# Loads at the start of a retention, ELU and max-out kernel: keys over all partitions, each weight half loaded once

## The chip, the cores and the metric

The kernel runs on one core of a Trainium2 chip. The metric is the device time of one execution in microseconds (us). Three executions of the kernel before took 1005.8, 998.84 and 1005.3 us, a median of 1005.3 us. A fourth execution was profiled and took 1000.28 us.

## The reference

Three stages follow one another. A retention layer runs over 4 sequences of 768 tokens with 8 heads of 64; its result goes, token by token, through a layer with ELU, and that result through a layer that takes the greatest of three projections.

```python
state = gamma * state + einsum('bhd,bhe->bhde', k[:, :, t], v[:, :, t])
y[:, :, t] = scale * einsum('bhd,bhde->bhe', q[:, :, t], state)
x = y.transpose(0, 2, 1, 3).reshape(3072, 512)
h = x @ moe_w_in                                    # 512 -> 2048
x = where(h > 0, h, exp(minimum(h, 0)) - 1) @ moe_w_out   # 2048 -> 512
h = maximum(maximum(x @ w1, x @ w2), x @ w3)        # 512 -> 768, three times
out = h @ moe2_w_out                                # 768 -> 512
```

The second and third stages' weights arrive as 64-bit numbers and are turned into pairs of 32-bit numbers on the chip.

## The kernel before

Retention runs in chunks of 128 tokens, 24 in all. The ELU layer runs over blocks of 512 tokens and over 16 slices of 128 hidden columns, numbered `f`. Products are made in three passes with a high and a low part of each operand.

**Chunks.** `load(c)` brings one chunk. The first eight (`early`, `EARLY` = 8) come from `qkv0`, where a row has five blocks of 128 numbers: queries of the first head of a pair, queries of the second head (each with zeros in the other head's rows), keys of both heads, keys by token, and values by token. In the tile `x`, slot 0 is for queries, slot 1 for keys, slot 3 for values; `rows(0)` are partitions 0 to 63, `rows(1)` are 64 to 127. Four transfers make up an early chunk: queries of `rows(0)`, keys of `rows(0)`, queries and keys of `rows(1)` in one (lines 110 to 114), and then the values over all partitions (line 127).

**Weight halves.** The 16 slices of the ELU layer's weights are loaded as 32 halves, numbered `n`, each of 128 rows of 4096 bytes (512 KB). `load_half(n)` chooses a place: `stage` (two buffers) or, for n = 2 to 5, a tile of the pool `ld` (two buffers with the tag `r`) that holds two halves, `duo`. A half is turned from 64 to 32 bits in steps: `scale` on ScalarE (line 307), `shift`, `sign` and `tail` on VectorE (lines 311, 317, 323), then `whigh` on ScalarE (line 341) and `wlow` on VectorE (line 346). The temporary `t` of a half has two buffers and is given back by `wlow`. Once `tail` is done, the place of a half is free, and `cv_tail` asks there for a later half (lines 327 and 328). In the first part of the kernel, which runs through `class Early`, `Early.tail` calls `cv_tail` and then asks for the same half itself (lines 1001 and 1002).

**Order.** SyncE (SP) issues all loads of chunks and halves in the order of the program, one after the other; an issue that waits holds back all behind it. The start is written out at line 845: chunks 0 and 1, half 0, chunks 2 and 3, half 1, chunk 4, halves 2 and 3, chunk 5, half 4, chunk 6, half 5, chunk 7. The string `ORDER` then gives the order of all steps of the first part for TensorE (PE), VectorE (DVE), ScalarE (ACT) and GpSimd (POOL); each engine runs its own steps in that order. Halves pass through `tail` in the order 0, 1, 2, 3, 4, 6, 5, 8, 7. Of `ORDER`, the stretch that matters reads:

```
mask6 fade7 scale6 shift6 sign6 tail6 hb2 exp2 relu2 score7:12 update7 mask7 middle7 oa0 oc0 ob0 whigh6
wlow6 ha3:0 hc3 hb3 whigh3 wlow3 scale5 oa1 oc1 ob1 state7 value7:12 near7 elu2 ghigh2 shift5 sign5 tail5
scale8 shift8 sign8 tail8 exp3 relu3 whigh5 oa2 wlow5 scale7 oc2 guard7 far7 high7 elu3 value6:03 near6
```

Here `ha`, `hb`, `hc` are the three passes of the ELU layer's first product for a slice (line 1080), `oa`, `ob`, `oc` those of its second product (line 1088); `turn`, `score`, `update`, `value`, `near`, `far`, `guard`, `mask`, `middle`, `state`, `keys` are steps of retention (`far` on PE is line 248 and its like, `guard` on ACT is line 973, `mask` on DVE line 203, `value` of the later chunks line 261). After `ORDER` the steady loop begins: `h1` (line 376) and `o1` (line 410) by turns.

Of the kernel before, what the change touches and what calls it, by code (L numbers as in the profile page):

```python
# [17 lines left out]
P = 128  # L18
# [13 lines left out]
NSTAGE = 2  # L32
# [25 lines left out]
def kernel(ctx: ExitStack, tc: tile.TileContext, qkv0, qkv, wa, wb, dmask, qdec, cols, out):  # L58
# [34 lines left out]
    def load(c, part=None):  # L93


        if c >= NCHUNK:
            return

        early = c < EARLY
        src = qkv0 if early else qkv  # L100
        if part != 1:
            if c in raw_t:
                return
            if early:
                x = wpool.tile([P, NPAIR, 4, P], F32, tag="w", name="x")
            else:
                x = ld.tile([P, NPAIR, 4, P], F32, tag="r", name="x")
            raw_t[c] = x
            if early:
                for h, at_, o, n in ((rows(0), 0, 0, 1), (rows(0), 1, 2, 1), (rows(1), 0, 1, 2)):  # L110
                    nc.sync.dma_start(
                        out=x[h, :, at_:at_ + n, :].rearrange("d p s t -> d p (s t)"),
                        in_=src[c, :, h, o * P:(o + n) * P].rearrange("p d t -> d p t"),
                    )
            else:
                for g in range(2):
                    for s in range(2):
                        for p in range(1 if c < 2 * NCH else 2):
                            ps = slice(None) if c < 2 * NCH else slice(p, None, 2)
                            cc = slice((2 * s + (g ^ p)) * P, (2 * s + (g ^ p) + 1) * P)  # L120
                            nc.sync.dma_start(
                                out=x[rows(g), ps, s, :], in_=src[c, ps, rows(g), cc].rearrange("p d t -> d p t")
                            )
        if part != 0:
            x = raw_t[c]
            if early:
                nc.sync.dma_start(
                    out=x[:, :, 3, :], in_=src[c, :, :, 4 * P:5 * P].rearrange("p t n -> t p n")
                )
            else:  # L130
                nc.sync.dma_start(
                    out=x[:, :, 2:4, :].rearrange("t p s n -> t p (s n)"),
                    in_=src[c, :, :, 4 * P:].rearrange("p t n -> t p n"),
                )
# [3 lines left out]
    def rows(i):  # L138
        return slice(i * HC, (i + 1) * HC)
# [149 lines left out]

    def load_half(n):  # L290
        if n < len(sources):
            if 2 <= n < 6:
                if n % 2 == 0:
                    duo[n // 2] = ld.tile([P, 2, 512, 2], I32, tag="r", name="raw")
                r = duo[n // 2][:, n % 2]
            else:
                r = stage.tile([P, 512, 2], I32, tag="raw", name="raw")
            nc.sync.dma_start(out=r.rearrange("p n w -> p (n w)"), in_=sources[n].bitcast(I32))
            half[n] = r
# [21 lines left out]
    def cv_tail(n):  # L321
        t = tmp[n].bitcast(U32)
        nc.vector.scalar_tensor_tensor(
            out=t, in0=half[n][:, :, 0].bitcast(U32), scalar=29, in1=t,
            op0=ALU.logical_shift_right, op1=ALU.bitwise_or,
        )
        if n < 2 or n >= 6:
            load_half(n + 6 if n < 2 else n + NSTAGE)

    def cv_rest(n):  # L330
        if n // 2 >= len(keys):
            return
        cv_shift(n)
        cv_sign(n)
        cv_tail(n)
# [179 lines left out]
    def words(src, t, loaded, freed):  # L515
# [20 lines left out]
        def tail():  # L536
# [3 lines left out]
            )  # L540

        get = Op("S", 0.0, load, *loaded)
        got = Op("A", 0.67, scale, (get, 2), *freed)
        Op("D", 0.42, shift, (got, 0))
        Op("D", 0.69, sign)
        return get, Op("D", 0.69, tail)

    def prepare(k, slot, prev):
# [296 lines left out]
    for c, n in ((0, None), (1, 0), (2, None), (3, 1), (4, 2), (None, 3), (5, 4), (6, 5), (7, None)):  # L845
        if c is not None:
            load(c)
        if n is not None:
            load_half(n)
# [19 lines left out]
    class Early:  # L869
# [128 lines left out]

        def tail(n):
            cv_tail(n)  # L1000
            if n < 2 or n >= 6:
                load_half(n + 6 if n < 2 else n + NSTAGE)

        def whigh(n):
            cv_high(n)
# [99 lines left out]
    def visit(c):  # L1105
        if c // CB not in x_t:
            new_x(c // CB)
        values(c)
        load(c + 2)
        open_chunk(c + 1)  # L1110
        finish(c)
        ready(c + 1)
# [15 lines left out]
    n = 2 * FIRST  # L1128
# [191 lines left out]
```

## Time and profile before

| | before |
|---|---|
| three executions | 1005.8, 998.84, 1005.3 us |
| median | 1005.3 us |
| profiled execution | 1000.28 us |
| its span, first to last instruction | 998.2 us |
| PE busy | 980.1 us (98%) |
| DVE busy | 607.1 us (61%) |
| ACT busy | 350.2 us (35%) |
| loads of weight halves | 37 of 512 KB |

A profile's page gives an engine's busy time over the whole span. The first 75 us, in which chunks and weights arrive, differ from the rest: they are the part that the change is in. The views of the trace that show them are the waits of an engine within a window, the chain of work that ended last in order of time, the timeline of one engine, and the table of windows with what the DMA engines moved.

### The profile page before, as it was taken

The page shows a single profiled execution, that of the slowest core. Times are in us where ns is not written, and L with a number is a line of the kernel's source. Part 1 is how long each engine was busy: PE and PEld are TensorE (multiplying, and loading weights), DVE is VectorE, ACT ScalarE, POOL GpSimd, SP SyncE. Part 2 cuts the span into 40 slices and gives each one's busy share as a digit, 9 for nine tenths or more (in the row PEclk, how much of TensorE's full clock was granted, in tenths as well). Part 3 has the DMA queues.
Part 4 walks back from the last instruction along what each step waited for, and adds up shares of the span by engine and source line. Part 5 has one row for each costly group of instructions (what it writes and reads, how often), then busy time and mean ns, then how long its engine had stood idle before and what let it go on. Part 6 is the DMA issues. An engine that isn't in the chain of part 4 may idle for free.

```text
span 998.2 us, 18878 instructions
## 1 busy us (share of the span) xinstructions
PE 980.1 (98%) x7820; PEld 848.6 (85%) x7820; DVE 607.1 (61%) x1137; ACT 350.2 (35%) x672; POOL 73.3 (7%) x84
## 2 busy tenths in 40 slices
PE   9889999999999999999999999999999999999998
PEld 6668887877887888888887888999999999999997
DVE  4766878544456655656654623676585765858654
ACT  2545665423443444444445433122121211212111
POOL 2200001021111111111110101000000000000000
PEclk9999999999999999999999999999999999999999
DMA  9943454344545554565556865402011020110101
GB/s 224 211 162 97 160 158 166 104 128 131 158 134 156 178 182 129 163 196 159 159 163 209 298 206 179 149 1 86 1 44 43 1 85 1 43 43 2 43 1 43
DMA packets 82308, 119.58 MB, mean 120 GB/s; under 512 B 6960, under 2 KB 59184, under 8 KB 79920
## 3 DMA queue, kind: packets, MB, share of 16 engines
q1 hardware_dynamic: 73008, 87.45, 29.8%
q0 software_dynamic: 3024, 19.66, 6.1%
q10 hardware_dynamic: 6192, 11.28, 3.2%
q8 instruction: 61, 1.00, 0.4%
q14 instruction: 23, 0.19, 0.1%
HBM read 84.02 MB, written 34.34 MB: 119 GB/s over the span
## 4 chain that ended last, share of the span: by engine, by line
PE 88%; DMA 6%; DVE 2%; ACT 2%; issue 1%; SPq 0%; ACTq 0%
PE hp L755 27%; PE acc L410 24%; PE hp L376 23%; PE acc L804 10%; DMA raw<-in_wa 3%; DMA x<-in_qkv 2%; PE xs L189 1%; PE xs L248 1%; PE xs L261 1%; PE xs L221 1%; DVE e L387 1%; DMA ops_d<-m 1%; PE bank L1088 1%; ACT gh L388 1%; ACT e L383 0%
## 5 line engine op out<-in xcount | busy, mean ns | idle before, releaser
L755 PE MATMUL hp<-xh,w 128*128 128x256 f32 x1512 | 275.0, 283 | 0.0
L755 PEld LDWEIGHTS hp<-xh,w 128*128 128x128 f32 x1512 | 237.0, 192 | 0.7
L376 PE MATMUL hp<-xh,w 128*128 128x512 f32 x736 | 235.8, 389 | 0.0
L755 PE MATMUL hp<-xl,w 128*128 128x256 f32 x756 | 213.9, 283 | 0.0
L410 PE MATMUL acc<-gh,w 128*128 128x512 f32 x736 | 194.4, 394 | 2.3 <-DVE part L435 0.9
L410 PEld LDWEIGHTS acc<-gh,w 128*128 128x128 f32 x736 | 135.7, 188 | 34.9 <-ACT gh L388 2.5
L376 PEld LDWEIGHTS hp<-xh,w 128*128 128x128 f32 x736 | 138.1, 188 | 28.8
L755 PEld LDWEIGHTS hp<-xl,w 128*128 128x128 f32 x756 | 145.1, 192 | 0.7
L387 DVE SCALAR_TENSOR_TENSOR e<-e,hp 128x512 f32<-128x512 f32 x92 | 63.0, 685 | 131.6 <-ACT e L384 131.2
L376 PE MATMUL hp<-xl,w 128*128 128x512 f32 x368 | 137.3, 389 | 0.0
L410 PE MATMUL acc<-gl,w 128*128 128x512 f32 x368 | 105.1, 390 | 0.0
L762 DVE TENSOR_TENSOR t<-hp,m 128x256 f32<-128x256 f32 (+1 forms) x108 | 55.0, 509 | 75.8 <-PE hp L755 75.3
L383 ACT ACTIVATE e<-hp 128x512 f32<-128x512 f32 x92 | 54.7, 594 | 123.0 <-PE hp L376 121.2
L391 DVE TENSOR_TENSOR gl<-e,gh 128x512 fp32r<-128x512 f32 x92 | 64.2, 698 | 49.0 <-ACT gh L388 47.5
L774 ACT COPY m<-hp 128x256 f32<-128x256 f32 x54 | 20.1, 373 | 198.3 <-PE hp L755 107.5
L388 ACT CAST gh<-e 128x512 fp32r<-128x512 f32 x92 | 57.1, 621 | 91.5 <-DVE e L387 91.5
L804 PE MATMUL acc<-w,gh 128*128 128x512 f32 x288 | 88.9, 390 | 0.0
L410 PEld LDWEIGHTS acc<-gl,w 128*128 128x128 f32 x368 | 69.1, 188 | 15.0 <-DVE gl L391 0.4
L376 PEld LDWEIGHTS hp<-xl,w 128*128 128x128 f32 x368 | 69.1, 188 | 14.4
L804 PEld LDWEIGHTS acc<-w,gh 128*128 128x128 f32 x288 | 54.1, 188 | 10.7
L384 ACT ACTIVATE e<-e 128x512 f32<-128x512 f32 x92 | 58.2, 633 | 2.9
L804 PE MATMUL acc<-w,gl 128*128 128x512 f32 x144 | 56.2, 391 | 0.0
(144 smaller groups left out, 990.7 us busy)
## 6 DMA issues: line engine op xcount, KB each, us to landing
raw<-in_wa SPq DMA_DIRECT2D x37, 512.0 KB, 3.7
w<-ops_d POOLq DMA_DIRECT2D x18, 1024.0 KB, 5.2
ops_d<-m SPq DMA_DIRECT2D x66, 256.0 KB, 3.0
raw<-in_wb SPq DMA_DIRECT2D x24, 512.0 KB, 4.4
x<-in_qkv SPq DMA_DIRECT2D x16, 512.0 KB, 4.3
x<-in_qkv SPq DMA_DIRECT2D x96, 64.0 KB, 2.5
raw<-x2d SPq DMA_DIRECT2D x10, 512.0 KB, 4.3
x<-in_qkv SPq DMA_DIRECT2D x32, 128.0 KB, 4.6
```

The lines of the kernel that those rows point to most:

```text
L189: nc.tensor.matmul(banks[g][rows(s), p, :], x[rows(g), p, 1, t], x[rows(g), p, 0, t], start=p == 0, stop=p == NPAIR - 1, skip_group_check= ...
L376: nc.tensor.matmul(hp, w[:, pw, kk * P:(kk + 1) * P], x[px][:, kk, :], start=k == 0, stop=k == len(order) - 1,)
L383: nc.scalar.activation(e, hp, ACTF.Exp)
L384: nc.scalar.activation(e, e, ACTF.Relu, scale=-1.0, bias=1.0)
L387: nc.vector.scalar_tensor_tensor(out=e, in0=e, scalar=-1.0, in1=hp, op0=ALU.mult, op1=ALU.max)
L388: nc.scalar.copy(gh, e)
L391: nc.vector.tensor_tensor(out=gl, in0=e, in1=f32(gh), op=ALU.subtract)
L410: nc.tensor.matmul(acc_t[b][m], w[:, p[0], 512 + m * P:512 + (m + 1) * P], g[p[1]], start=f == f0 and p == first, stop=f == f1 - 1 and p = ...
L755: nc.tensor.matmul(o, ws[i][:, pw, kk * P:(kk + 1) * P], xs[i][px][:, kk, :], start=first and k == 0, stop=last and k == 5,)
L762: nc.vector.tensor_tensor(out=out, in0=a, in1=c, op=ALU.add)
L774: nc.scalar.copy(u, pa[:, :HB])
L804: nc.tensor.matmul(acc_t[NB + b][m], g[px][:, m * P:(m + 1) * P], w[:, pw, :], start=f == 0 and i == 0, stop=f == KF2 - 1 and i == 2,)
```

## The change

Three edits. In `load`, an early chunk still comes by four transfers, but the cut is another: queries of `rows(0)`, queries of `rows(1)`, and keys over all 128 partitions in one; values as before. A packet is then always one row of 512 bytes, where queries and keys of `rows(1)` came in rows of 1024 bytes.

`Early.tail` no longer asks for a half, so that `cv_tail` alone does.

`load_half` puts halves 8 and 9 into a `duo` tile of the pool `ld`, where halves 2 and 3 were, and `cv_tail` asks for them once half 3 has passed `tail`. Halves 6 and 7 ask for 10 and 11 when they have passed, 8 and 9 ask for nothing, and from 10 on each asks for the one two further, as before. `ORDER` is not changed.

```diff
             if early:
-                for h, at_, o, n in ((rows(0), 0, 0, 1), (rows(0), 1, 2, 1), (rows(1), 0, 1, 2)):
+                for h, at_, o in ((rows(0), 0, 0), (rows(1), 0, 1), (slice(None), 1, 2)):
                     nc.sync.dma_start(
-                        out=x[h, :, at_:at_ + n, :].rearrange("d p s t -> d p (s t)"),
-                        in_=src[c, :, h, o * P:(o + n) * P].rearrange("p d t -> d p t"),
+                        out=x[h, :, at_, :], in_=src[c, :, h, o * P:(o + 1) * P].rearrange("p d t -> d p t")
                     )
...
-            if 2 <= n < 6:
+            if 2 <= n < 6 or n in (8, 9):
...
-        if n < 2 or n >= 6:
-            load_half(n + 6 if n < 2 else n + NSTAGE)
+        if n < 2:
+            load_half(n + 6)
+        elif n == 3:
+            load_half(8)
+            load_half(9)
+        elif n in (6, 7):
+            load_half(n + 4)
+        elif n >= 10:
+            load_half(n + NSTAGE)
...
         def tail(n):
             cv_tail(n)
-            if n < 2 or n >= 6:
-                load_half(n + 6 if n < 2 else n + NSTAGE)
```

## Rows read from the trace of the kernel before

**Rows 1.** The page: the span.

```profile
span 998.2 us, 18878 instructions
```

**Rows 2.** The page, DMA issues: count, KB of each, median us from issue to landing.

```profile
raw<-in_wa SPq DMA_DIRECT2D x37, 512.0 KB, 3.7
```

**Rows 3.** Waits of PE from 5 to 76 us: us in total, times, longest.

```profile
PE bank L1088 <- ACT w L341: 2.2, 1, 2.2
PE bank L984 <- ACT xh L980: 2.1, 2, 1.4
PE bank L221 <- DVE room L203: 1.6, 1, 1.6
PE bank L1088 <- issue: 1.5, 1, 1.5
...
PE bank L873 <- DMA x<-in_qkv: 0.4, 1, 0.4
```

**Rows 4.** Window 90 to 140: length, each engine's busy time (instructions), clock, DMA share, GB/s.

```profile
90.00:140.00 50.00, 50.00 (x222) 41.42 (x221) 39.67 (x67) 30.14 (x53) 0.00 (x0) 1.00 0.45 144
```

**Rows 5.** Chain that ended last, 0 to 80 us: start, us, what (DMA: issue to landing).

```profile
40.38 8.41 DMA raw<-in_wa
48.80 3.98 DMA raw<-in_wa
...
55.46 4.98 DMA raw<-in_wa
...
60.46 3.71 DMA raw<-in_wa
...
64.25 0.66 ACT t L307
...
66.62 2.12 PE bank L1088 x8
```

**Rows 6.** Waits of SP, 0 to 80 us: us in total, times, longest.

```profile
SPq L298 <- DMA raw<-in_wa: 27.5, 6, 7.2
```

**Rows 7.** Timeline of DVE: start, us, what; in brackets the idle time before.

```profile
53.50 0.43 DVE L311 TENSOR_SCALAR t<-t 128x512 int32<-128x512 int32 x1 [0.54 <-ACT t L307]
...
59.60 0.69 DVE L323 SCALAR_TENSOR_TENSOR t<-raw,t 128x512 uint32<-128x512 uint32 x1
64.94 0.43 DVE L311 TENSOR_SCALAR t<-t 128x512 int32<-128x512 int32 x1 [4.64 <-ACT t L307]
```

**Rows 8.** Timeline of ACT, the same columns.

```profile
58.60 0.62 ACT L1034 CAST gh<-e 128x512 fp32r<-128x512 f32 x1 [0.91 <-DVE e L1028]
64.25 0.66 ACT L307 ACTIVATE t<-raw 128x512 f32<-128x512 f32 x1 [5.03 <-DMA raw<-in_wa]
```

**Rows 9.** Timeline of PE, the same columns.

```profile
56.19 0.73 PE L1088 MATMUL bank<-gh,w 128*128 128x512 f32 x2 [1.55 <-issue]
...
59.51 1.07 PE L1080 MATMUL bank<-xl,w 128*128 128x512 f32 x4
...
63.23 0.69 PE L261 MATMUL bank<-room,x 64*64 64x64 f32 x32
```

**Rows 10.** Six windows of the loads, with the columns of rows 4.

```profile
14.00:16.50 2.50, 2.50 (x40) 1.99 (x36) 1.68 (x4) 1.14 (x2) 0.05 (x1) 1.00 1.20 199
16.50:17.50 1.00, 1.00 (x27) 0.93 (x24) 0.97 (x2) 0.47 (x1) 0.23 (x1) 1.00 1.22 255
...
34.30:35.40 1.10, 1.10 (x7) 0.91 (x6) 1.03 (x3) 0.74 (x2) 0.25 (x1) 1.00 1.13 198
21.00:22.80 1.80, 1.80 (x21) 1.44 (x23) 0.98 (x2) 0.00 (x0) 1.19 (x1) 1.00 1.07 320
39.60:41.50 1.90, 1.15 (x48) 1.01 (x48) 1.83 (x3) 0.65 (x2) 0.62 (x1) 1.00 1.14 228
42.00:43.00 1.00, 0.65 (x22) 0.52 (x26) 0.62 (x2) 1.00 (x2) 0.00 (x0) 1.00 1.15 184
```

**Rows 11.** DMA queues from 53 to 56 us: packets, MB, share.

```profile
q8 instruction: 1, 0.02, 2.1%
```

## Prediction

> **What bounds the kernel now.** I read the page first, then PE's waits before and after the start, then the chain in order of time, then the timelines of the engines along that chain, and last the windows of the loads.
>
> The span is 998.2 us [rows 1], and TensorE (PE) is busy in nearly all of it. From 90 to 140 us it is busy for 50.00 us of 50.00 [rows 4]: behind the start, PE's own work sets the pace. So a load counts only where PE waits for it, and time won there moves everything behind it forward by the same amount. PE's waits from 5 to 76 us are seven rows, of which the first four and the last are shown; the seven add up to 9.7 us [rows 3]. This is the ceiling for a change that touches only loads.
>
> Next, what the waits come from. The chain from 40 us on is made of weight halves: one lands at 48.79, the next is issued at 48.80 and lands 3.98 us later, a third is issued at 55.46, and a fourth, issued at 60.46 when the third has landed, lands 3.71 us later, just before ScalarE (ACT) begins `scale8` at 64.25 [rows 5]. By the code these are the first and the second copy of half 6 and of half 8: the first copy's buffer, that nobody reads, is filled again once the transfer is in. The page counts 37 loads of halves [rows 2] where the program has 32 halves; the five too many are the second copies of 6, 7, 8, 9 and 10. The queue of SyncE (SP) waited 27.5 us for earlier halves [rows 6], though that is no cost by itself.
>
> **Second copies, removed.** Half 6 lands about 4 us earlier (48.79 for 52.79). That is worth little: VectorE (DVE) idled only 0.54 us before `shift6` [rows 7], and the steps ahead of it keep it busy. PE waits for none of this, so I cost it at nothing.
>
> Half 8 is the one that counts. Its first copy had to wait for `tail6` and is issued at 55.46. ACT then idled 5.03 us before `scale8` [rows 8]; behind `scale8` in ACT's order stand `exp3`, `relu3` and `whigh5`, and PE's `oa2` at 66.62 waited 2.2 us for `whigh5` [rows 3, 5]. In the changed kernel half 8 goes out behind half 7, since `tail3` is long done. If half 6 lands at 48.79 as its first copy does now, halves 7 and 8 follow at about 1.6 us each (0.524 MB at 320 GB/s [rows 10]), so half 8 is in by 52 us and half 9 by 54. I then follow ACT: `ghigh2` ends at 58.60 + 0.62 = 59.22 [rows 8], `scale8` takes 0.66 and ends at 59.9. `exp3` needs the last matmul of `hb3`, 59.51 + 1.07 = 60.58 [rows 9]. `exp3` and `relu3` take about 0.62 each (as `ghigh2` does) and bring 61.8, by when `tail5` is done (59.60 + 0.69 = 60.29 [rows 7]); `whigh5` ends at 62.4. PE arrives at `oa2` at 66.62 - 2.23 = 64.4, behind `value7` (63.23 [rows 9]) and `near7`. So `whigh5` is 2.0 us early, and the wait goes: **2.2 us**. What is late next on PE is PE itself. DVE's idle 4.64 us before `shift8` [rows 7] goes too, so that `tail8` and `tail7` run ahead of PE. The second copies of 7, 9 and 10 lie on no wait of PE: nothing. What hides them is PE's own products; without these, each would cost about 4 us (3.71 to 3.98 [rows 5]).
>
> **Keys over all partitions.** The issue count stays at four a chunk, so SP's issue work doesn't change. Queries and keys took 512 KB over half the partitions at a time; now 256 KB of keys go like the values, over all. The trace of before has no such transfer of keys; the nearest row is the values'. From 14.0 to 16.5 us, where queries and keys of chunk 2 move, the DMA engines bring 199 GB/s; from 16.5 to 17.5, where its values move, 255 [rows 10]. For 0.262 MB that is 1.32 us against 1.03: 0.29 us a chunk. The bounds are from other windows: 198 and 320 GB/s (the second has weights in it) give 1.32 - 0.82 = +0.50 us, and 228 and 184 give 1.15 - 1.42 = -0.27 us, a loss [rows 10]. I take 0.29, since it compares neighbours of one chunk with no weights between them.
>
> How much of it does PE see? PE's wait of 1.6 us for `mask5` [rows 3] is the last that loads set before the second copies: `mask5` stands behind `tail4` on DVE, and `tail4` behind half 4, which six chunks precede on SP. From there PE has work to 54.2 us without a wait of this kind. So six chunks count: 6 x 0.29 = **1.7 us**, between 6 x (-0.27) = -1.6 and 6 x 0.50 = 3.0. Chunks 6 and 7 move earlier as well and aren't waited for.
>
> The Trainium skill, on its page "SBUF — State Buffer", section "Door 1: The DMA port swizzle", says that 64 partitions reach only half of the ports, with 196 GB/s against 328 at 1 MiB; by it the edit would give 0.54 us a chunk, an estimate, and the sum below would be 5.4 us for 3.9. The windows [rows 10] show the half's rate as stated and a smaller gain beside it. Against the change speaks "DMA: Bandwidth & Descriptors", section "Why small descriptors are slow (HBM only)": a fixed overhead of some 3 cycles a packet, so that rows of 512 bytes cost about 9% more than those of 1024, an estimate; that would take about 0.1 us a chunk off, and the sum would be 3.3 us.
>
> **New places.** Half 8 waits for `tail3` on SP, and behind it stand halves 9, 10 and 11. The first copy of half 6 is issued only at 40.38 [rows 5], and `tail3` is by `ORDER` ahead of `tail4`, which released `mask5` at about 42 us: no wait. Block 0's parked sums now take the place of halves 4 and 5, free since `tail5` at 60.29, and are written only when `ORDER` ends, at about 75 us. Halves 10 and 11 go out after `tail6` and `tail7`, earlier than now. All of this I cost at nothing; if one of these places were late, PE would wait about one load of 3.7 to 5.0 us [rows 5].
>
> **A wait that I leave.** PE idles 1.55 us before 56.19 and no semaphore ends it ("issue") [rows 9]; in that stretch one block of instructions is loaded [rows 11]. The likeliest is that PE waits for code. I leave it; bounds are 0 and 1.5 us of gain.
>
> **Sum.** 2.2 + 1.7 = 3.9 us. Against the profiled execution, 1000.28 - 3.9 = 996.4 us, a span of 994.3. But the four executions shown lie at two levels, 998.84 and 1000.28 against 1005.3 and 1005.8; no row says why. Their middle is 1002.8, and 1002.8 - 3.9 = **998.9 us**. I predict that.
>
> **Rivals.**
> *The loads were hidden anyway.* Only part of the 2.2 us comes, because PE meets another wait in its place, and keys gain nothing since windows of 184 GB/s occur over all partitions too. For it: a half 4 us earlier gains DVE only 0.54. Against it: `whigh5` has 2.0 us to spare. Gain 0 to 2 us, 1001.8.
> *All waits of the start go.* Faster chunks also free `high` (2.1 us [rows 3]) and the code wait. Gain 9.7 us, 993.1. Against it: half 2, which `high` stood behind, has only five chunks ahead, 1.5 us.
> *Slower: code comes late.* The loads now stand closer together, halves 6 to 9 behind each other; if the block of code queues behind them as half 6 did (8.41 us from issue to landing [rows 5]), asked for at 53 us it comes at 61.4 and PE restarts 5.2 us later than 56.19. It decides from a restart at 58.4 on (2.2 us later). Without a gain from keys this gives 5.2 - 2.2 = +3.0, 1005.8. Against it: by 54 us the halves are in.
>
> **How the numbers follow.** My forecast has 0.60, the hidden loads 0.20, all waits gone 0.12, late code 0.08. The range: below, the lowest execution less all bounds, 998.84 - (2.2 + 3.0 + 1.5) = 992.1, cut to 992.5; above, the highest less the smallest gain, 1005.8 - (2.2 - 1.6) = 1005.2, cut to 1005. A measurement of this kernel tells about 1%, 10 us, from no change. Only all waits gone comes near that; with the two levels falling well I give faster 0.09. Slower needs late code and bad levels together: 0.03. Within 1%: 0.88.
>
> **What would show it.** 32 loads of halves on the page. No wait of `oa2` for `whigh5`. `scale8` following `ghigh2` without a DMA between. PE's first `h1` near 71.5 us instead of 75.3. Queries and keys of a chunk landing 0.3 us sooner, `mask5` about 1.7 us sooner. Wrong if PE still waits for L341, if the halves land later than 59 us, if windows with keys bring under 200 GB/s, or if the time behind 76 us changes by more than 1 us.

## The result and the profile after

| | before | changed |
|---|---|---|
| median of 6 executions each | 1002.84 us (998.84 to 1005.8) | 993.2 us (992.36 to 995.33) |
| profiled execution | 1000.28 us | 993.02 us |
| its span | 998.2 us | 990.9 us |
| its mean granted clock of PE | 0.999 | 0.999 |

The ratio of the times is 0.9912, with an interval of 0.9884 to 0.994: the gain is clear of noise, and lies within the 1% to which the prediction gave 0.88. The time is inside the predicted range of 992.5 to 1005, near its lower end, and the gain is more than the 3.9 us forecast: 7.3 us between the two profiled spans and 9.6 us between the medians.

First the page of the changed kernel: the span, and the loads of halves with their count and median time from issue to landing (before: [rows 1, 2]).

```profile
span 990.9 us, 18871 instructions
...
raw<-in_wa SPq DMA_DIRECT2D x32, 512.0 KB, 4.0
```

The five second copies are gone, as the diff says. Next PE's waits from 5 to 76 us in the changed kernel, with the total, times and longest (before: [rows 3]). New line numbers: 1092 for 1088, 990 for 984, 220 for 221.

```profile
PE bank L220 <- DVE room L202: 1.8, 1, 1.8
PE bank L887 <- DMA x<-in_qkv: 1.2, 2, 0.7
PE bank L990 <- ACT minus_one L1074: 0.3, 1, 0.3
PE bank L247 <- ACT room L979: 0.3, 1, 0.3
```

Of 9.7 us, 3.6 are left. The wait of `oa2` for `whigh5`, the 1.5 us with no releaser and nearly all of the wait for `xh` are gone. The wait for `mask5` (now line 202) stays, and is 1.8 us where it was 1.6. The table of windows shows where the time came from: length, then busy time (instructions) of PE, PEld, DVE, ACT and POOL, granted clock, share and GB/s of the DMA engines. The kernel before:

```profile
0.00:20.00 20.00, 17.86 (x177) 11.40 (x177) 8.72 (x17) 4.45 (x8) 4.61 (x8) 1.00 1.05 216
20.00:40.00 20.00, 16.44 (x262) 13.20 (x259) 14.16 (x26) 7.91 (x16) 5.93 (x6) 1.00 1.13 254
40.00:60.00 20.00, 16.89 (x319) 13.32 (x314) 15.92 (x30) 10.31 (x23) 3.36 (x4) 1.00 0.66 178
60.00:80.00 20.00, 17.77 (x176) 14.31 (x175) 8.71 (x15) 8.97 (x22) 0.00 (x0) 1.00 0.41 132
```

and the changed kernel:

```profile
0.00:20.00 20.00, 17.34 (x177) 11.19 (x177) 9.82 (x17) 4.64 (x8) 5.59 (x9) 1.00 1.04 249
20.00:40.00 20.00, 17.79 (x324) 14.59 (x325) 16.57 (x31) 9.70 (x19) 5.13 (x6) 1.00 1.15 285
40.00:60.00 20.00, 20.00 (x309) 16.12 (x308) 17.28 (x32) 11.51 (x26) 3.12 (x3) 1.00 0.31 115
60.00:80.00 20.00, 19.99 (x142) 15.73 (x141) 10.73 (x19) 11.27 (x25) 0.00 (x0) 1.00 0.09 27
```

In the first 40 us the loads run at 249 and 285 GB/s where they had 216 and 254, with an equal share of busy DMA engines. From 40 to 80 us PE is idle for 0.01 us, before for 5.34. The timelines of PE give the end of it: start, duration, line, and the first `h1` before and then after.

```profile
75.29 0.39 PE L376 MATMUL hp<-xh,w 128*128 128x512 f32 x1
```

```profile
67.53 0.39 PE L382 MATMUL hp<-xh,w 128*128 128x512 f32 x1
```

The loop starts at 67.53 us, 7.76 us earlier, where 71.5 was forecast. If the same products of PE are followed through both traces, the lead grows in three steps. The product that starts at 39.63 us before starts 3.86 us earlier. The lead is 3.59 us up to the product at 54.24; `oa` at 56.19 starts 5.31 us earlier, so 1.72 come with the idle time without a releaser. `oa2` at 66.62 starts 7.76 us earlier, another 2.45. After the first `h1` the lead stays between 7.3 and 7.8 us to the end.

### The profile page after: what moved, and what is told of

Same layout as the page of the kernel before. It is cut to its first block, busy times and chain, and to the rows that moved or that the text cites. A ratio compares the mean times of both kernels' runs of the same rounds, so it can differ in the third digit from the quotient of the medians.

```text
span 990.9 us, 18871 instructions
## 1 busy us (share of the span) xinstructions
PE 978.2 (99%) x7820; PEld 848.2 (86%) x7820; DVE 607.4 (61%) x1137; ACT 350.0 (35%) x672; POOL 73.2 (7%) x84
## 4 chain that ended last, share of the span: by engine, by line
PE 92%; DVE 3%; DMA 2%; ACT 2%; issue 1%; SPq 0%; ACTq 0%
PE hp L761 27%; PE acc L416 24%; PE hp L382 23%; PE acc L810 10%; DMA x<-in_qkv 1%; PE bank L1092 1%; PE xs L188 1%; PE xs L247 1%; PE xs L260 1%; PE xs L220 1%; PE bank L1084 1%; DMA ops_d<-m 1%; DVE e L393 1%; ACT gh L394 1%; DVE t L316 0%
## 5 line engine op out<-in xcount | busy, mean ns | idle before, releaser
L382 PEld LDWEIGHTS hp<-xl,w 128*128 128x128 f32 x368 | 69.1, 188 | 14.4
```

What stands on the lines that cost most here:

```text
L382: nc.tensor.matmul(hp, w[:, pw, kk * P:(kk + 1) * P], x[px][:, kk, :], start=k == 0, stop=k == len(order) - 1,)
```

## The experiments

### One part at a time

**keys_only**: the kernel before with the new cut of the early chunks, and nothing else of the change.

```diff
-                for h, at_, o, n in ((rows(0), 0, 0, 1), (rows(0), 1, 2, 1), (rows(1), 0, 1, 2)):
+                for h, at_, o in ((rows(0), 0, 0), (rows(1), 0, 1), (slice(None), 1, 2)):
```

> The kernel before with the new cut of queries and keys alone; halves are loaded twice as before. Theory A (the share of bytes that goes to 64 partitions sets the time of a chunk, about 1.1 us less a chunk and half from one landing to the next): half 4 lands about 5 us before 38.72, the products of retention that wait for it (before at 39.63) come 3.5 to 4 us earlier, and the steady loop, which began at 75.3 us, begins at 71.4 to 72; the waits of PE for whigh5 (2.2 us) and for code (1.5 us) stay. About 4 us faster than before. Rival B (the earlier end of the loads came from the removed second copies, which no longer load the DMA engines): less than 1 us faster, since all chunks stand ahead of the second copies on SP.

Measured: 999.93 us median (998.08 to 1001.62) beside 1004.63 of the kernel before, ratio 0.9956 [0.9936, 0.9976]. The product that starts at 39.63 us before starts at 36.24 here: the new cut alone moves PE by 3.39 us there, twice the 1.7 of my term and close to the whole change's 3.86. The two longest of PE's waits from 5 to 76 us in this kernel:

```profile
PE bank L1087 <- ACT w L340: 2.1, 1, 2.1
PE bank L220 <- DVE room L202: 1.8, 1, 1.8
```

The wait for `whigh5` stands as before, so that part belongs to the second copies. The idle time without a releaser is not there, though the copies are. In this execution two stretches in which PE's clock was halved took back about 3.4 us (placed below, under "The kernel before once more"), so the span of 997.8 us understates the edit, and the steady loop begins at 73.18 us, not at the 71.4 to 72 that were expected.

**single_only**: the changed kernel with the old cut of the chunks.

```diff
-                for h, at_, o in ((rows(0), 0, 0), (rows(1), 0, 1), (slice(None), 1, 2)):
+                for h, at_, o, n in ((rows(0), 0, 0, 1), (rows(0), 1, 2, 1), (rows(1), 0, 1, 2)):
```

> The changed kernel with the old cut of queries and keys; halves are loaded once, 8 and 9 in the new places. Theory A: up to 50 us PE runs as before (the products at 39.63 within 0.5 us of it), PE's wait for whigh5 is gone (2.2 to 2.5 us won), and the steady loop begins at 72 to 73 us. On the wait for code: if code queues behind loads, halves 6 to 9 now stand closer together and land by about 54 us, so a wait of 1 to 3 us stays near 54 us; if the second copies alone made it, it is gone and the loop begins at 71.5. Rival B: the chunks too come 3 to 5 us earlier.

Measured: 997.68 us (994.89 to 1001.04), ratio 0.992 [0.9894, 0.9946]. Half 4 lands at 39.92 us, where the profile of before had 38.72 and that of the changed kernel 33.68; the product that started at 39.63 starts at 40.84. So nothing is gained before 41 us without the new cut. PE's waits from 5 to 76 us, complete:

```profile
PE bank L221 <- DVE room L203: 2.0, 1, 2.0
PE bank L880 <- DMA x<-in_qkv: 1.7, 2, 1.2
PE bank L888 <- DMA x<-in_qkv: 1.4, 2, 0.8
PE bank L991 <- ACT xh L987: 1.1, 1, 1.1
PE bank L248 <- ACT room L980: 0.4, 1, 0.4
```

The wait for `whigh5` is gone with the copies, as expected. The steady loop begins at 75.35 us and not at 72 to 73: PE ran at half its clock for 10.2 us in this execution, which was the slowest of the four. The one of 994.89 us ran at a mean clock of 1.0.

**What follows.** The two parts are separate in the traces: the cut gives 3.4 to 3.9 us by 40 us, the copies some 2.3 us at `oa2`. Neither half of the change is idle. The medians don't split in the same way. `keys_only` gains 4.7 us (2.4 to 6.4 by its interval) and `single_only` 7.0 (5.4 to 10.6), which is more than the wait of 2.2 us that it removes, and together they make 11.7 where the whole change has 9.6. The mean clock of the eight executions of the kernel before beside them is 0.9951 and that of `single_only` 0.9975, about 2.4 us over 1000; the rest of the difference stays open.

### The new places, and the code

**old_places**: the changed kernel with halves 8 and 9 back in `stage`, asked for after `tail6` and `tail7`, each still loaded once.

```diff
-            if 2 <= n < 6 or n in (8, 9):
+            if 2 <= n < 6:
...
+        if n < 2 or n >= 6:
+            load_half(n + 6 if n < 2 else n + NSTAGE)
```

> The changed kernel with halves 8 and 9 in the two stage buffers as before, asked for after tail6 and tail7 (10 after tail8, 11 after tail9), each once. Theory A: half 8 is issued at about 51.2 us and lands 3.5 us later at 54.7 to 55, within 0.3 us of where scale8 stood in the changed kernel (54.91); half 9 lands by 65 us for a use at about 73. The steady loop begins within 0.5 us of 67.5 us: the places are worth almost nothing, the single copy all. Rival: half 8 lands later than 56 us, oa2 waits again for over 1 us, and the loop begins at 68.5 us or later.

Measured: 994.01 us in one execution, span 991.9. Half 8 is issued at 52.59 and lands at 56.38, about 11 us later than in the changed kernel (45.28), and PE still does not wait for `whigh5`. It lands later than expected (54.7 to 55 us), and the loop begins at 68.88 us for 67.53, which is what the rival had forecast, but for another reason: the 1.35 us are lost from 39.6 to 43 us, where PE's clock was halved in this execution, and from there to the loop nothing more is lost. So this one trace shows no worth in the new places; dropping the second copies is what counts.

**extra_loads**: the changed kernel with four more loads of 256 KB, which nobody reads, right behind half 9.

```diff
             load_half(9)
+            for pool, tag, bufs in ((dpool, "m", 2), (dpool, "m", 2), (at, "a", 1), (at, "qd", 1)):
+                extra = pool.tile([P, 512], I32, tag=tag, name="extra", bufs=bufs)
+                nc.sync.dma_start(out=extra, in_=sources[0][:, 0:256].bitcast(I32))
```

> The changed kernel with four more loads of 256 KB each (1 MB, into tiles that nothing reads) issued right behind half 9. Theory C (a block of PE's code queues behind the loads that already stand on the DMA engines): the code block that moved at 46.98 us, just after half 9 had landed at 46.52, moves only when the extra loads have landed, at 49.5 to 51 us, and PE waits 1 to 3 us for code near 50 us, so that the steady loop begins at 68.5 to 70.5 us in place of 67.5. Rival D (code is fetched when PE reaches a place in its program, whatever the DMA engines do): the block moves at 47 us again, no wait, and the loop begins at 67.5 us.

Measured: 992.55 us in one execution, span 990.7. The extra loads land from 47.0 to 49.0 us; the block of instructions moves at 46.76, as in the changed kernel (46.98), and PE doesn't wait. 1 MB more of loads ahead of the code cost nothing in this execution, which speaks against queueing behind loads as the cause of the idle 1.55 us of [rows 9].

### How the cut works

**short_rows** and **short_grouped**: the changed kernel with queries and keys again to 64 partitions at a time, in four transfers of 128 KB with rows of 512 bytes. The first orders them by slot, the second by half of the partitions.

```diff
-                for h, at_, o in ((rows(0), 0, 0), (rows(1), 0, 1), (slice(None), 1, 2)):
+                for h, at_, o in ((rows(0), 0, 0), (rows(1), 0, 1), (rows(0), 1, 2), (rows(1), 1, 2)):
```

```diff
+                for h, at_, o in ((rows(0), 0, 0), (rows(0), 1, 2), (rows(1), 0, 1), (rows(1), 1, 2)):
```

> The changed kernel with keys cut by partitions again: four transfers of 128 KB, each to 64 partitions in rows of 512 bytes, in place of two of 128 KB and one of 256 KB over all. Theory A (64 partitions are what is slow): half 4 lands at 38 to 40 us as before the change (38.72) and the products at 35.77 us move back to 39 to 41. Rival E (rows of 1024 bytes to 64 partitions were what was slow): half 4 lands within 1 us of 33.7 as in the changed kernel.

> As short_rows (four transfers of 128 KB to 64 partitions in rows of 512 bytes), but in the order of the kernel before: both of one half, then both of the other. In short_rows half 4 landed at 36.95 us, 1.8 us before the kernel before (38.72). If the shorter rows did that, half 4 lands at 36.5 to 37.5 again; if the change of halves from one transfer to the next did, it lands at 38.5 to 40.5 as in the traces with the old cut.

Measured: one execution each, 994.07 us (span 992.1) and 996.55 us (span 994.6). Half 4 lands at 36.95 and 37.83 us, between the two forecasts of either run; with the old cut it landed at 38.72, 39.92 and 40.38 in three traces, with the new one between 33.45 and 34.92 in four. Shorter rows show no cost, and more than half of the gain (3.4 of 5.7 us at half 4, by the means of these) is lost when keys go to 64 partitions at a time, though these two kernels also have one transfer more in a chunk. Whether the rest, 2.3 us, comes from the shorter rows, from the order or from the spread between executions, one execution each doesn't settle.

**wide**: the changed kernel with queries and keys of an early chunk in one transfer of 512 KB over all partitions, from an array in which the queries of both heads are stacked without the zeros. The place of the values in that array moves with it, which the cut below leaves out. A chunk now has two transfers in place of four, and rows of 1024 bytes again.

```diff
...
+                nc.sync.dma_start(
+                    out=x[:, :, 0:2, :].rearrange("d p s t -> d p (s t)"),
+                    in_=src[c, :, :, 0:2 * P].rearrange("p d t -> d p t"),
+                )
...
```

> The changed kernel with queries and keys of an early chunk in one transfer of 512 KB over all 128 partitions, rows of 1024 bytes; the two heads' queries stand in one block in memory, without the zeros that no product reads. Theory A (bytes sent to 64 partitions move at about 140 GB/s, those over all at about 340, by the two steps from landing to landing before and after): a chunk and a half take 3.6 to 3.8 us in place of 4.7, half 4 lands near 27 us in place of 33.68, and PE's waits of 5 to 70 us, 3.6 us after the change, shrink to 1 to 2 us. The steady loop begins at 65 to 66 us in place of 67.5; 1.5 to 2.5 us faster than the changed kernel, 0.989 to 0.991 of the kernel before. Rival (the gain came from fewer or shorter packets in some other way, rows of 1024 bytes cost more): half 4 lands at 32 us or later, and the time is that of the changed kernel.

Measured: 991.63 us (990.61 to 994.33), ratio to the kernel before 0.989 [0.987, 0.991]. Half 4 lands at 27.66 us, 6 us ahead of the changed kernel's. But PE's waits are now 2.5 us in all, with this one as their core:

```profile
PE bank L220 <- DVE room L202: 1.8, 1, 1.8
```

So the loads are no longer what `mask5` is late for; the next section asks what is. The waits didn't shrink to 1 to 2 us as expected, and the loop begins at 66.48 us, not at 65 to 66: behind the wait for `mask5` stands a stretch of 3.4 us at half clock.

### The last wait of the start

`scale4` on ACT begins as soon as half 4 is in, in the kernel before and in the changed one; behind it stand `shift4`, `sign4`, `tail4` and `mask5` on DVE.

```profile
38.80 0.67 ACT L307 ACTIVATE t<-raw 128x512 f32<-128x512 f32 x1 [2.70 <-DMA raw<-in_wa]
```

```profile
33.76 0.68 ACT L306 ACTIVATE t<-raw 128x512 f32<-128x512 f32 x1 [0.99 <-DMA raw<-in_wa]
```

In the changed kernel the timeline of DVE (start, duration, line, operation, what; idle time before in brackets) around `mask5` reads:

```profile
34.88 0.68 DVE L898 TENSOR_TENSOR kd<-bank,cols_sb 128x512 f32<-128x512 f32 x1
35.48 0.46 DVE L310 TENSOR_SCALAR t<-t 128x512 int32<-128x512 int32 x1
35.98 1.64 DVE L316 SCALAR_TENSOR_TENSOR t<-raw,t 128x512 int32<-128x512 int32 x1
37.65 0.69 DVE L322 SCALAR_TENSOR_TENSOR t<-raw,t 128x512 uint32<-128x512 uint32 x1
38.26 0.75 DVE L202 TENSOR_TENSOR room<-bank,dmask_sb 128x256 f32<-128x256 f32 x2
```

and that of POOL in the same kernel:

```profile
35.62 1.45 POOL L949 TENSOR_TENSOR room<-x,qdec_sb 128x512 f32<-128x512 f32 x1
```

`sign4` (line 316) takes 1.64 us where its median is 0.69, and begins while POOL's product of queries is under way, which ends at 37.07; from there `sign4` needs 0.55 us. The Trainium skill, on its page "SBUF — State Buffer", section "Who interferes with whom", says that a DVE instruction with two inputs in SBUF contends with a GpSimd instruction that reads SBUF. `sign4` reads `raw` and `t`, and the trace agrees. In the kernel before `sign4` took 0.69 us, since POOL's product was over by then (38.95 + 1.27 = 40.22); there `shift4` stood beside it and took 1.00 us for 0.43 to 0.46:

```profile
38.95 1.27 POOL L943 TENSOR_TENSOR room<-x,qdec_sb 128x512 f32<-128x512 f32 x1
39.50 1.00 DVE L311 TENSOR_SCALAR t<-t 128x512 int32<-128x512 int32 x1 [0.60 <-ACT room L973]
40.54 0.69 DVE L317 SCALAR_TENSOR_TENSOR t<-raw,t 128x512 int32<-128x512 int32 x1
41.87 0.75 DVE L203 TENSOR_TENSOR room<-bank,dmask_sb 128x256 f32<-128x256 f32 x2
```

So POOL's product holds DVE up in both kernels, by about 0.55 us before and 0.95 after. Half 4 itself no longer sets `mask5` in the changed kernel: `scale4` ends at 34.44, and DVE is at earlier steps until 35.48.

**wide_order**: `wide`, with `sign4` and `tail4` moved behind `mask5` in `ORDER`. It ran beside **wide_again** and **after_again**, which are `wide` and the changed kernel once more, on the same chip.

```diff
-keys5 scale4 shift4 sign4 tail4 value4:14 near4 guard4 far4 high4 score5:36 mask5 update5 middle5 query5
+keys5 scale4 shift4 value4:14 near4 guard4 far4 high4 score5:36 mask5 sign4 tail4 update5 middle5 query5
```

> Queries and keys in one transfer over all partitions (as in wide), and in ORDER the steps sign4 and tail4 moved behind mask5. The wait of PE for mask5 (1.8 us after the change, 1.8 in wide) then comes from DVE's order and not from a load: half 4 has been in for 5 us there. Theory: the wait shrinks to under 1 us, with it one reason for TensorE's clock to fall near 39 us, and the kernel is 1 us faster than wide, 3 us faster than the changed kernel. Rival: the wait moves to the next step that needs tail4 or whigh4, or stays as long because GpSimd's product at that time slows DVE, and the time is that of wide.

> wide once more, on one chip with the changed kernel: if its 2.2 us in the profile are real, its median stands 1 to 3 us under that of the changed kernel; if the clock's falls and the waits behind 76 us use them up, the two agree within 1 us.

> The changed kernel once more, beside the next two on one chip, for its time against theirs and a second trace: 0.989 to 0.993 of the kernel before; half 4 lands at 33 to 35 us.

Measured: `wide_order` 988.99 us (988.26 to 989.78), ratio to the kernel before 0.9858 [0.9838, 0.9878]; `wide_again` 991.78 (990.51 to 996.6), 0.9896 [0.9876, 0.9916]; `after_again` 993.81 (991.88 to 994.24), 0.9905 [0.9886, 0.9923]; the kernel before 1003.34. All the waits of PE in `wide_order` from 5 to 76 us, and then DVE around `mask5`:

```profile
PE bank L220 <- DVE room L202: 0.5, 1, 0.5
PE bank L247 <- ACT room L979: 0.3, 1, 0.3
```

```profile
35.11 0.76 DVE L202 TENSOR_TENSOR room<-bank,dmask_sb 128x256 f32<-128x256 f32 x2 [1.05 <-PE bank L188]
35.79 0.68 DVE L316 SCALAR_TENSOR_TENSOR t<-raw,t 128x512 int32<-128x512 int32 x1
```

`sign4` runs behind POOL's product in 0.68 us, and `mask5` waits for PE's scores alone. The edit takes the two steps themselves, 0.69 us each, out of the way of `mask5` as well as the 0.95 us of POOL's product, so it doesn't separate these. This version beats both kernels: 4.8 us under the changed one by medians, 14.4 under the one before. Of the 2.8 us against `wide`, 1.3 are the shorter wait for `mask5`; the traces of `wide` and `wide_again` also have 3.4 and 6.8 us at half clock behind that wait, and this one has none. Whether `wide` is faster than the changed kernel (about 2 us by medians) their overlapping intervals leave open.

### The kernel before once more, and PE's clock

**before_again**: the kernel before, unedited, for a second trace.

> The kernel before once more, for a second trace. If its times spread because TensorE's granted clock falls to half in some stretches of the first 80 us, this execution shows such stretches, and its span is longer than 998.2 us by half of their length (3 to 7 us of half clock cost 1.7 to 3.4 us). If PE's wait for code near 54 us belongs to the kernel, it is there again with 1 to 2 us and the code block moves late, at about PE's 720th product; if it belongs to that execution alone, the block moves at about the 650th, as in the other kernels, and no such wait is listed.

Measured: 1003.93 us, span 1001.8. Two of PE's waits from 5 to 76 us:

```profile
PE bank L1088 <- ACT w L341: 3.6, 1, 3.6
PE bank L881 <- DMA x<-in_qkv: 3.1, 3, 2.1
```

The wait for `whigh5` is 3.6 us here, against 2.2 in the first trace, and PE shows no idle row between 47 and 64 us: the 1.55 us before 56.19 don't recur. They are absent from `keys_only` and `single_only` too. What PE waited for in that one execution stays open.

The table of windows of this execution, with the granted clock in the third column from the right:

```profile
35.80:39.20 3.40, 3.40 (x10) 2.66 (x9) 3.00 (x6) 1.49 (x3) 1.16 (x1) 0.50 1.13 205
69.90:73.30 3.40, 3.40 (x50) 2.54 (x51) 2.68 (x5) 0.96 (x5) 0.00 (x0) 0.50 0.49 154
```

and of `single_only`:

```profile
29.80:33.20 3.40, 3.40 (x58) 2.74 (x58) 1.84 (x4) 0.66 (x2) 1.27 (x1) 0.50 1.18 208
43.50:50.30 6.80, 6.30 (x86) 5.01 (x87) 3.22 (x8) 3.12 (x7) 0.00 (x0) 0.50 1.01 325
```

In these stretches PE ran at 1.2 of its 2.4 GHz. Each stands in or shortly behind a gap: PE had waited 1.83 us to 34.48 and 3.59 us to 68.86 in `before_again`; in `single_only` it waited 2.01 us to 44.00, and 1.05 and 0.50 us to 27.89 and 29.51. `keys_only` has two such stretches, behind the waits of 1.8 and 2.1 us. The wait alone doesn't decide it. The wait of 1.8 to 2.0 us for `mask5` has a stretch at half clock at its end or shortly behind it in `keys_only`, `old_places`, `short_grouped`, `wide` and `wide_again`, and none in both traces of the changed kernel, in `extra_loads` and in `short_rows`; the first profile of before has waits of 1.6, 1.55 and 2.2 us and no stretch. By these traces a stretch of 3.4 us costs an estimated 1.7 us at most, half its length; the one of `old_places` cost PE 1.35.

## Why the prediction came out as it did

**Second copies: right.** `oa2` gained 2.45 us where 2.2 was the term. What was forecast to show it shows on ACT's timeline of the changed kernel (before: [rows 8]): `scale8` stands right behind `ghigh2` with no load between.

```profile
54.38 0.62 ACT L1038 CAST gh<-e 128x512 fp32r<-128x512 f32 x1 [0.91 <-DVE e L1032]
54.91 0.67 ACT L306 ACTIVATE t<-raw 128x512 f32<-128x512 f32 x1
```

Halves 6, 7, 8 and 9 landed at 42.76, 44.03, 45.28 and 46.52 us, half 6 thus 6 us ahead of my estimate, since the chunks in front of it were quicker.

**Keys: the step that failed.** The mechanism was right in the main and the size wrong. I priced 0.29 us a chunk by two windows of [rows 10], taking the window of values for a window of transfers to 128 partitions. Such windows are no pure samples, and the packets in the trace show it: all 498 data packets from 16.5 to 17.5 us have 512 bytes, but counted in the order of the queue only some 243 of them can be values, and the rest are queries and keys of the next chunk, to 64 partitions. The window of 184 GB/s, which gave the bound of a loss, has 85 packets of 1024 bytes, and only queries and keys of `rows(1)` have those.

A better measure is the step from one landing to the next. Between the landings of halves 1 and 2, 3 and 4, 4 and 5, one chunk and one half go through: 5.60, 6.03 and 6.05 us before, mean 5.89; 4.72, 4.70 and 4.99 after, mean 4.80. That is 1.09 us a chunk; `before_again` and `after_again` give 5.76 and 4.81, or 0.95. These steps aren't quite pure either: a chunk and a half are 1.311 MB, and the queue moved 1.62, 1.34 and 1.36 MB in the three of before, the first with most of half 3 in it.

How much of this comes from the partitions is less sure. Before, 0.524 MB go to 64 partitions and 0.786 MB to 128 in such a step; after, 0.262 and 1.049. If that is the whole difference, twice the second less the first is 3.71 us for 1.311 MB to 128 partitions, some 350 GB/s; the rest gives (5.89 - 0.786 x 2.83) / 0.524 = 7.0 us per MB, some 143 GB/s, for 64. `wide` fits: 1.311 MB a step to 128 partitions should take 3.71 us, and its three took 3.68, 4.05 and 3.76, though with fewer transfers. But the two kernels with short rows send the same 0.524 MB to 64 partitions, and their five steps took 5.12 to 5.64 us, mean 5.41. With 5.41 for 5.89 the same working gives some 310 and 180 GB/s, both estimates, and the window of 14.0 to 16.5 us, in which no packet of weights moves, has 199 [rows 10]. So some 0.6 us of the 1.09 belong to keys over all partitions, and what in the old cut made the other 0.5 stays open.

Over the six chunks ahead of half 4 the landing came 5.04 us sooner (0.84 a chunk, as the first four gain only 2.49 together), and `mask5` 3.61 us sooner on DVE, from 41.87 to 38.26. Of the 1.43 us between the two, 1.02 went because DVE was still at earlier steps when half 4 was in, and 0.41 because POOL's product now held up `sign4` by 0.95 us, where it had held up `shift4` by 0.55. My upper bound, 3.0 us, was below the result; a bound built from windows of the same mixed kind bounds little. The Trainium skill's "SBUF — State Buffer", section "Door 1: The DMA port swizzle", gave 0.54 us a chunk, an estimate by its own figures, nearer to the 1.09 than mine and close to the 0.6 that the short rows leave to the partitions. The objection by short rows fell: neither kernel with short rows was slower for them.

**The rival "all waits of the start go".** It was closer than my forecast: the median of 993.2 us is its 993.1, and 6.1 of the 9.7 us of waits went, the wait for `xh` among them, which I had set aside because half 2 has only five chunks ahead of it, at 0.29 us each. Half 2 landed 3.37 us sooner. That the median meets its number is in part chance, since the wait for `mask5` stayed and a part of the gain by medians may be clock. **Late code** and **hidden loads** fell.

**The code wait: left in, gone.** I left its 1.55 us; the comparison of the two profiles has 1.72 us of gain there. But in a second trace of the kernel before it is gone as well, so I count it neither to the change nor against it. Without it the gain by the two profiles is 5.6 us and not 7.3, against the 3.9 of the sum.

**The new places: nothing, as forecast.** `old_places` shows it, in one execution.

**The range.** It held, but not because the sum was right: 998.9 us was forecast and 993.2 measured. Its lower end started from the lowest of four executions and took every bound off it. The signs named ahead came out for the copies (32 loads, `scale8` behind `ghigh2`, no wait for `whigh5`) and missed by about twice for the keys (first `h1` at 67.53 us for 71.5, `mask5` 3.61 us sooner for 1.7).

**The two levels of the times.** The prediction took the middle of the four executions without knowing a reason. By the later traces the times go with PE's granted clock and with load waits that vary. Eleven executions of the kernel before in the last comparison have a mean clock of 0.9957, the changed kernel's four beside them 0.9988; over 1000 us that is 3 us of work at full speed, about what the gain by medians (9.6) has over the gain by profiles (7.3). That the shorter waits cause the higher clock is likely from where the stretches stand, but wasn't shown by taking one wait away. One execution of the kernel before took 1003.34 and another 999.68 us at the same mean of 0.998, so the clock isn't all.

## What to carry to other kernels

Price a transfer by the steps from one landing to the next, and count the bytes and packets that move in them; GB/s in a window in which several kinds are under way tells little of any one kind. A run that changes little but the partitions is worth more than a fit of two rates. Where a queue of loads sets the start, a new cut for 256 KB of each chunk was worth nearly a fifth of a step here (1.09 of 5.89 us), and each wait that disappears uncovers the next, here DVE's order with a product of POOL beside it. Profile the kernel before twice ahead of a forecast of a few us: waits of 1.5 us, and stretches at half clock that cost up to 1.7 us, came and went between executions.

## What the runs showed of the hardware

- The cut that moves 256 KB of a chunk over all 128 partitions and not over 64 at a time took 0.95 to 1.09 us off a step of 5.8 to 5.9 us in one queue; against cuts with equally short rows it was 0.6 us.
- PE's clock fell to 1.2 GHz in stretches of the first 75 us, in some executions and not in others, behind waits of 0.5 to 3.6 us; a stretch of 3.4 us cost 1.35 us in `old_places`.
- A product of DVE over two SBUF operands took 1.64 us for 0.69 when it began during POOL's product of 1.45 us, and a shift over one operand took 1.00 us for 0.43 beside POOL's product of 1.27.
- 1 MB of additional loads in the queue ahead of a block of instructions didn't delay that block (46.76 against 46.98 us), in one execution.
